# Crossbar transposes for two head pairs of batch 1, and a new order of copies in the prologue, in a fused attention + feed-forward kernel

## The chip, the core and the metric

The kernel runs on one core of one Trainium2 chip. The metric is the device time of one execution in microseconds (us). Every kernel here was executed several times; one execution carries the profile. A profile's *span*, from the first to the last instruction, is about 2 us shorter than the device time of the same execution. A run is called *slow* when it is over 1.5% above the fastest run of the same kernel; slow runs are kept out of the comparisons.

The engines are TensorE (PE in the profile; PEld is its weight load), VectorE (DVE), ScalarE (ACT), GpSimd (POOL) and SyncE (SP; SPq is its queue of DMA issues). Each works through its own list of instructions in a fixed order; the kernel's author chose the orders by hand, so an instruction whose data are late holds up all that stand behind it on that engine.

## The reference

```python
# q, k, v: (4, 8, 768, 64); block = 32, window = 16
k_sum = k.reshape(B, H, nb, block, D).max(axis=3)      # one key per block: the maximum
v_sum = v.reshape(B, H, nb, block, D).mean(axis=3)     # one value per block: the mean
scores_l = scale * q @ k^T          # kept only where |i - j| < 16
scores_s = scale * q @ k_sum^T + log(block)
a = softmax(concat(scores_l masked, scores_s))
x = a @ concat(v, v_sum)            # then (B*S, H*D) = (3072, 512)
h = x @ w_in                        # 512 -> 2048
out = (h * sigmoid(beta * h)) @ w_out   # 2048 -> 512
```

## The kernel before

Heads are worked on in pairs: 4 batches with 4 pairs each. While TensorE does the feed-forward product of batch b (`h_ps`, then `o_ps`), the attention of batch b+1 is slipped in between as "side" work, at positions fixed by numbers. Batch 0's attention is the prologue. For every pair of the next batch the side work is:

1. `copy_v` (a copy of the values on GpSimd) and `prep_v`: the values' block means on TensorE (`vm_ps`), evicted by VectorE (`vm`), and four small copies that SyncE issues as DMAs to put rows and means in place.
2. `transposes`: keys and queries are transposed. Batches 2 and 3 let the DMA crossbar do it (`dma_start_transpose`), issued by SyncE. Batch 1 lets TensorE do it (`pt`), and ScalarE evicts.
3. `rows_a` and `rows_b` on VectorE: the keys' tile `kw` gets extra rows (block maxima `km`, window edges). The crossbar delivers chunks in another order than TensorE's transposes do, so rows after a crossbar transpose take more and smaller copies (the branch `b > 1`).
4. `scores`, `mask`, `av`, `norm` (`x_nat`, VectorE), `x_transpose` (`px`, TensorE in batch 1).

```python
def prep_v(b, g):
    ...                                                    # vm_ps on TensorE
    nc.vector.tensor_copy(out=vm..., in_=...)              # (cut: ScalarE in one case)
    overlaps(b, g, nc.sync)                                # two small DMAs
    eng.dma_start(out=ve[SUM[0]:SUM[0] + nb], in_=vm[:])   # two more; eng is nc.sync
    eng.dma_start(out=vo[SUM[1]:SUM[1] + nb, :, 1:], in_=vm[:])

def transposes(b, g, i):                                   # i = 0 keys, 1 queries
    ...
    if b > 1:
        nc.sync.dma_start_transpose(out=dst, in_=src)
        return
    pt = ps.tile([P, nch, P], bf16, name="pt", tag="t", bufs=2)
    for n in range(nch):
        for h in range(2):
            nc.tensor.transpose(pt[h * D:(h + 1) * D, n], nat[(b, g)][i][:, h * nch + n], identity)
    nc.scalar.copy(out=dst, in_=pt[:])

# the side work of the next batch, for pair g (batch 0 is in its feed-forward part):
t = (16.0, 18.5, 21.5, 24.5)[g]
st, sp, sc_t, av_t = t + 1.3, t - 0.6, (t + 4.6, t + 5.6), t + 9.4
side += [(t - 0.7, copy_v), (t, transposes of keys), (t + 1.2, transposes of queries),
         (st, rows_a and rows_b), (sp, prep_v), (av_t, av), (av_t + 1.2, norm),
         (av_t + 2.3, x_transpose)]                        # (lambdas cut)

# batch 2's loads on GpSimd may not be issued before batch 1's last rows are done:
tc.add_manual_dep(first[(2, 0)].ins, last[(1, npair - 1, "rows")].ins.name, ...)
```

On VectorE, the rows of pair 3 (25.8) stand ahead of the normalisation of pair 0 (26.6). On SyncE, a pair's transposes (t) stand behind its four value copies (t - 0.6). The last line ties batch 2's loads to the rows of pair 3.

The softmax here doesn't subtract the row's maximum and nothing guards it: scores larger than these inputs give would overflow.

## Time and profile before

| | before |
|---|---|
| device time, median of 3 runs | 232.47 us (231.98 to 233.33) |
| span of the profiled run | 230.6 us |
| TensorE busy | 92% of the span |
| first `h_ps` of batch 1 | 87.11 us |
| `px` of pair 0, batch 1 | 72.78 us |
| first load of batch 2 on GpSimd | 71.58 us |

From the page of before: the line of busy time (engine, us, share of the span, instructions), TensorE's busy tenths in 40 slices of the span, and the clock that TensorE was granted in the same slices, in tenths of full speed (9 is 90% or more).

```profile
PE 211.2 (92%) x1969; PEld 118.0 (51%) x1969; DVE 105.6 (46%) x278; ACT 125.4 (54%) x149; POOL 77.1 (33%) x109
PE   0689799997999999999799999999999999999992
PEclk9999999999999999999999999999999999999999
```

TensorE bounds the kernel: after the first slices it is full, so what holds TensorE up costs time, unless a later wait gives some of it back. The waits of TensorE between 45 and 135 us say how little it was held up (instruction, whom it waited for, total us, times, longest):

```profile
PE o_ps L395 <- DVE vm_128 L207: 1.4, 1, 1.4
```

This is the longest. It lies in batch 2 at 114 us. The next longest, 0.9 and 0.8 us, are one for an eviction by ScalarE and one for batch 1's first key load, at 51.5 us.

The timelines have the start, the duration, the engine, the source line, the operation, out<-in, the count, and in brackets the idle time just before with what ended it. SyncE's queue of DMA issues:

```profile
65.46 0.65 SPq L195 DMA_DIRECT2D vo_124<-ve_122  x1
66.19 0.62 SPq L196 DMA_DIRECT2D ve_122<-vo_124  x1
66.90 1.04 SPq L212 DMA_DIRECT2D ve_122<-vm_127  x1
67.99 0.83 SPq L213 DMA_DIRECT2D vo_124<-vm_127  x1
```

These are pair 2's four value copies: each occupies SyncE for 0.6 to 1.0 us just to issue, some 3.5 us for a pair, and SyncE is without a gap from 58.2 us on. VectorE, TensorE and GpSimd at the same time:

```profile
70.82 0.29 DVE L298 COPY kw_120<-km 128x144 bf16<-128x144 bf16 x2
...
71.28 0.96 DVE L350 TENSOR_TENSOR x_nat<-av_ps,r 128x768 bf16<-128x768 f32 x1
```

```profile
71.24 0.35 PE L315 MATMUL s_ps<-q_tr,kw_119 64*128 64x64 bf16 x12
...
72.78 0.51 PE L364 MATMUL px<-identity,x_nat 128*128 128x128 bf16 x6
```

```profile
71.58 1.02 POOL L185 DMA_DIRECT2D ve_121<-in_v_dram  x1 [6.21 <-DVE r L349]
```

Pair 3's rows end at 71.0, the normalisation of pair 0 follows at once, TensorE's `px` follows that without a wait, and GpSimd starts batch 2's loads 0.6 us after pair 3's rows.

### The profile page before, as it was taken

To read this page: it belongs to the slowest core of one execution; us is meant where nothing else is said; L and a number is where in the kernel's file an instruction comes from. 1 tells how busy PE (TensorE), PEld (TensorE's weight loads), DVE (VectorE), ACT (ScalarE), POOL (GpSimd) and SP (SyncE) were. 2 spreads that over 40 slices of the span, in tenths; PEclk is the share of its full clock that TensorE was granted. 3 is DMA by queue.
4 is the path that set the end of the run, shared out by engine and by line. 5 is a ranking of instruction groups with operands and counts; after the bars stand their busy time and mean duration, and the time that the engine had idled before them with its cause. 6 is when DMAs were issued, how large, how long until landed. Compare 5 with 4: busy or idle time off the path is not lost.

```text
span 230.6 us, 4864 instructions
## 1 busy us (share of the span) xinstructions
PE 211.2 (92%) x1969; PEld 118.0 (51%) x1969; DVE 105.6 (46%) x278; ACT 125.4 (54%) x149; POOL 77.1 (33%) x109
## 2 busy tenths in 40 slices
PE   0689799997999999999799999999999999999992
PEld 0456565654545555666344546665445456654441
DVE  4798630545577520598784405766543200002121
ACT  2567886672786537666934237667644177660000
POOL 6999963446415993673560000000000000000000
PEclk9999999999999999999999999999999999999999
DMA  6986599999967999999998339343134410001212
GB/s 177 347 251 145 86 165 205 206 170 156 150 105 104 182 177 210 190 145 141 160 180 158 84 80 173 67 89 62 63 82 110 132 47 0 0 3 45 91 58 80
DMA packets 93254, 29.25 MB, mean 127 GB/s; under 512 B 79792, under 2 KB 89560, under 8 KB 93232
## 3 DMA queue, kind: packets, MB, share of 16 engines
q0 software_dynamic: 61424, 13.76, 69.6%
q1 hardware_dynamic: 28688, 14.02, 27.1%
q10 hardware_dynamic: 3120, 1.18, 1.9%
q8 instruction: 15, 0.25, 0.5%
q14 instruction: 7, 0.06, 0.1%
HBM read 27.27 MB, written 6.29 MB: 146 GB/s over the span
## 4 chain that ended last, share of the span: by engine, by line
PE 64%; DMA 19%; POOL 8%; DVE 3%; SPq 2%; ACT 1%; issue 1%; POOLq 0%; ACTq 0%
PE o_ps L395 34%; PE h_ps L380 23%; DMA k_nat<-in_k_dram 8%; DMA q_tr<-q_nat 4%; DMA w_in_sb<-in_moe_w_in_dram 3%; DMA hold_83<-in_v_dram 3%; PE av_ps L339 3%; PE s_ps L315 2%; POOL ve_121 L175 2%; POOL vo_123 L175 1%; PE pt L251 1%; PE vm_ps L202 1%; POOL hold_83 L81 1%; DVE vm_128 L207 1%; SPq L246 1%
## 5 line engine op out<-in xcount | busy, mean ns | idle before, releaser
L395 PE MATMUL o_ps<-w_out_sb,h_sb 128*128 128x512 bf16 x384 | 88.9, 380 | 1.6 <-DVE vm_128 L207 1.4
L380 PE MATMUL h_ps<-xT,w_in_sb 128*128 128x384 bf16 x512 | 85.5, 326 | 0.1
L384 ACT ACTIVATE h_sb<-h_ps,beta_sb 128x768 bf16<-128x768 f32 x64 | 57.2, 900 | 24.9 <-PE h_ps L380 24.8
L380 PEld LDWEIGHTS <-w_in_sb 128*128 128x128 bf16 x512 | 49.7, 98 | 32.4 <-issue 0.3
L395 PEld LDWEIGHTS <-h_sb 128*128 128x128 bf16 x384 | 35.1, 98 | 40.5 <-issue 1.5
L318 ACT ACTIVATE attn<-s_ps,bias 128x768 bf16<-128x768 f32 x32 | 28.4, 900 | 15.7 <-PE s_ps L315 15.6
L399 DVE COPY o_sb<-o_ps 128x512 f32<-128x512 f32 x6 | 4.2, 692 | 42.1 <-PE o_ps L395 42.1
L399 ACT COPY o_sb<-o_ps 128x512 f32<-128x512 f32 x18 | 10.5, 585 | 23.3 <-PE o_ps L395 21.9
L324 DVE TENSOR_TENSOR attn<-attn,band 128x768 bf16<-128x768 bf16 x24 | 15.2, 638 | 15.3 <-ACT attn L318 15.3
L185 POOL DMA_DIRECT2D k_nat<-in_k_dram x12 | 12.4, 1037 | 11.9 <-DMA kw_120<-k_nat 4.6
L350 DVE TENSOR_TENSOR x_nat<-av_ps,r 128x768 bf16<-128x768 f32 (+1 forms) x17 | 15.4, 910 | 0.6
L185 POOL DMA_DIRECT2D q_nat<-in_q_dram x12 | 12.4, 1032 | 7.5 <-DMA q_tr<-q_nat 3.2
L160 DVE TENSOR_SCALAR w_out_sb<-w_out_sb,inv_beta 128x512 bf16<-128x512 bf16 x16 | 6.1, 436 | 12.9 <-DMA w_out_sb<-in_moe_w_out_dram 12.9
L185 POOL DMA_DIRECT2D ve_122<-in_v_dram x8 | 8.2, 1031 | 4.5 <-DMA w_in_sb<-in_moe_w_in_dram 1.9
L202 PEld LDWEIGHTS <-A_avg 128*128 128x128 bf16 x96 | 7.1, 102 | 5.2 <-issue 3.2
L339 PEld LDWEIGHTS <-attn 128*64 128x64 bf16 x384 | 7.4, 110 | 4.4 <-issue 3.4
L266 DVE COPY kw_117<-kw_117 128x480 bf16<-128x480 bf16 x2 | 0.6, 284 | 19.7 <-DMA kw_117<-k_nat 19.7
L349 DVE RECIPROCAL r<-av_ps 128x12 f32<-128x12 f32 x16 | 3.6, 224 | 11.8 <-PE av_ps L339 11.8
L190 POOL COPY vo_124<-ve_122 128x768 bf16<-128x768 bf16 x8 | 7.2, 894 | 4.9 <-DMA ve_122<-in_v_dram 4.9
L226 PE MATMUL pk<-identity,k_nat 128*128 128x128 bf16 x24 | 3.0, 288 | 6.1 <-POOL k_nat L169 5.9
L365 ACT COPY xT<-px 128x768 bf16<-128x768 bf16 x7 | 5.6, 798 | 3.2 <-PE px L364 3.2
L202 PE MATMUL vm_ps<-ve_121,A_avg 128*128 128x128 bf16 x48 | 4.6, 240 | 2.1 <-POOL ve_121 L175 2.0
(165 smaller groups left out, 201.0 us busy)
## 6 DMA issues: line engine op xcount, KB each, us to landing
out_dram<-o_sb SPq DMA_DIRECT2D x24, 256.0 KB
k_nat<-in_k_dram POOLq DMA_DIRECT2D x12, 192.0 KB, 9.6
q_nat<-in_q_dram POOLq DMA_DIRECT2D x12, 192.0 KB, 10.4
w_out_sb<-in_moe_w_out_dram POOLq DMA_DIRECT2D x4, 512.0 KB, 16.2
w_in_sb<-in_moe_w_in_dram POOLq DMA_DIRECT2D x3, 512.0 KB, 9.9
ve_122<-in_v_dram POOLq DMA_DIRECT2D x8, 192.0 KB, 12.8
hold_81<-in_k_dram POOLq DMA_DIRECT2D x2, 384.0 KB, 5.3
hold_82<-in_q_dram POOLq DMA_DIRECT2D x2, 384.0 KB, 4.8
```

The lines of the kernel that those rows point to most:

```text
L175: copy(out=t[:, :, :, 0:D], in_=f)
L185: ins = nc.gpsimd.dma_start(out=dst, in_=src[b, g])
L190: nc.gpsimd.tensor_copy(out=vo[:, :, 1:, 0:D], in_=ve[:, :, :, 0:D])
L202: nc.tensor.matmul(vm_ps[:], A_avg[:, c, :], ve[:, :, c, 0:D], start=(c == 0), stop=(c == nch - 1))
L318: nc.scalar.activation(out=a.rearrange("p i n q -> p i (n q)"), in_=big[:, :, 0:w], func=ACTF.Exp, bias=bias[:, par:par + 1], scale=scale)
L324: nc.vector.tensor_mul(out=a, in0=a, in1=band[:, par, None, None, :].to_broadcast([P, 2, nch, QT]))
L339: nc.tensor.matmul(o[par * QT:(par + 1) * QT, h, m * HW:(m + 1) * HW], a[:, par, i, n], vt[par][:, h, m], start=True, stop=True)
L350: nc.vector.tensor_mul(out=x_nat[(b, g)][:, lo:hi].rearrange("p m h d -> p h m d"), in0=ov[:, :, lo:hi, 0:D], in1=r_of[(b, g)][:, :, lo:hi ...
L380: nc.tensor.matmul(big[:, kk, 0:MG], w_in_sb[:, ki, ni * P:(ni + 1) * P], xT[b][:, ki, kk * MG:(kk + 1) * MG], start=(ki == 0), stop=(ki = ...
L384: nc.scalar.activation(out=h_bufs[(b, ni // 8)][:, ni % 8, :].rearrange("p (k m) -> p k m", k=2), in_=big[:, :, 0:MG], func=ACTF.Silu, sca ...
L395: nc.tensor.matmul(o_ps[:], h_bufs[(b, ni // 8)][:, ni % 8, ms * P:(ms + 1) * P], w_out_sb[:, ni, :], start=(ni == 0), stop=(ni == k2 - 1))
L399: (nc.scalar.copy if b + 1 < B else nc.vector.tensor_copy)(out=o_sb[:], in_=o_ps[:])
```

## The change

The change has two parts.

*Prologue (batch 0).* The second copy of the keys, which VectorE made with a reduce, is now written by ScalarE straight from PSUM (the memory of the kernel's `ps` tiles, which TensorE's results go to), and pair 0's rows are put ahead of a cast on VectorE. Some later steps of the prologue are reordered.

*Crossbar (batch 1).* Pairs 2 and 3 take the path of batches 2 and 3: SyncE's crossbar transposes instead of 12 TensorE transposes and a ScalarE eviction for each of two tiles of each pair. The intent is to take 48 transposes off the engine that bounds the kernel.

```diff
+        nc.scalar.copy(out=kw_bufs[g][:, 1, :, QT - W:P].rearrange("p m (f e) -> p m f e", e=NE),
+                       in_=pk.rearrange("p e (m f) -> p m f e", f=P // NE)[:, :, (QT - W) // NE:])
 ...
+    def by_parity(b, g):
+
+        return b > 1 or (b == 1 and g >= 2)
 ...                                     # in transposes; the same swap in rows_a, rows_b and av
-        if b > 1:
+        if by_parity(b, g):
             nc.sync.dma_start_transpose(out=dst, in_=src)
 ...
-            if b == 2:
+            if not by_parity(b - 1, g):
                 nc.vector.memset(kv[D:P, 1, :, nj - 1, 0:W], 0.0)
 ...
-            cv(out=kw[:, 1, :, QT - W:P], in_=kw[:, 0, :, QT - W:P])
+            if b:
+                cv(out=kw[:, 1, :, QT - W:P], in_=kw[:, 0, :, QT - W:P])
 ...                                     # the order of the prologue
     pool_0()
-    cast_qk("k", 1, dve)
     prep_k(0)
     prep_q(0)
     rows_a(0, 0)
+    cast_qk("k", 1, dve)
 ...
-    sc(2)
+    scores(0, 2, 0)
+    prep_q(3)
+    scores(0, 2, 1)
+    av(0, 1)
     rows_a(0, 3)
     rows_b(0, 3)
-    prep_q(3)
     sc(3)
-    fin(1)
+    norm(0, 1)
+    av(0, 2)
+    norm(0, 2)
     x_transpose(0, 0)
+    x_transpose(0, 1)
 ...                                     # (two more moved lines cut)
```

More of the change, by code (lines that the diff above doesn't have):

```diff
@@ L262, in rows_a @@
         km = at_pool.tile([P, nb], bf16, name="km", tag="km")
-        if b > 1:
+        if by_parity(b, g):
             kv = kw.rearrange("p r (h j) f -> p r h j f", h=2)
@@ L280, in rows_b @@
         kw, km = kw_bufs[(b * npair + g) % NKW], kms.pop((b, g))
-        if b > 1:
+        if by_parity(b, g):
             kv = kw.rearrange("p r (h j) f -> p r h j f", h=2)
@@ L336, in av @@
             for m in range(nch):
-                i, n = (m % 2, h * nj + m // 2) if b > 1 else (h, m)
+                i, n = (m % 2, h * nj + m // 2) if by_parity(b, g) else (h, m)
                 for par in range(2):
@@ L466 @@
     rows_b(0, 2)
+    prep_k(3)
     fin(0)
-    prep_k(3)
     prep_v(0, 3)
@@ L475 @@
         load_next(1, g)
-    sc(2)
+    scores(0, 2, 0)
+    prep_q(3)
+    scores(0, 2, 1)
+    av(0, 1)
     rows_a(0, 3)
     rows_b(0, 3)
-    prep_q(3)
     sc(3)
-    fin(1)
+    norm(0, 1)
+    av(0, 2)
+    norm(0, 2)
     x_transpose(0, 0)
+    x_transpose(0, 1)
     nc.vector.tensor_copy(out=identity32[:], in_=identity[:])
-    fin(2)
-    x_transpose(0, 1)
     load_beta()
```

## The prediction

> **What bounds the kernel now.** The page's busy table gives TensorE 92% of 230.6 us; by stretches it is full from 70 us to the end but for one 1.4 us wait near 114 us. The chain of waits runs through GpSimd in the head (8 to 26 us), then DMA: a w_in load, and batch 1's first k_nat, which lands at 52.24 us. TensorE's last h_ps matmul of batch 0 ends by 51.0, so the prologue already has slack against that load.
>
> **Prologue part.** Per pair VectorE drops a 128x480 reduce (0.64 us) and ScalarE gains a 480-column copy (estimate 0.56 us, from its 0.59 us for 512). Pair 0's rows no longer stand behind the 1.23 us k cast. I expect h_ps to start 0 to 1 us before 29.35. GpSimd's order does not change, so the loads do not move; k_nat still lands near 52.2 and the gain becomes a longer wait there. Worth: about 0.
>
> **Batch 1 part.** Removed: four groups of 12 TensorE transposes (0.46 us each, 1.85 us), some 0.5 us of waits around them, and four ScalarE copies of 0.80 us. Added: four crossbar transposes on SyncE's queue. In the timeline of before, SyncE issues without a gap from 58.2 to 72.6 us (four value copies per pair, about 3.5 us a pair). The built order puts pair 2's transposes after pair 2's value copies, so they cannot start before about 68.9. In batch 3, with quiet DMA, VectorE could use a transpose 2.8 us after its issue began (147.41 to 150.26), and the rows of this layout take 3.0 us instead of 1.9. In the built order:
> - Pair 2's keys land at 71.7, rows done 74.8. Its first scores (71.24 in before, about 69 without the removed work) wait: a hole of 6 us.
> - VectorE copies pair 3's value means after these rows: 75.7 (68.0 in before).
> - SyncE's copies of those means stand before pair 3's key transpose: issue 77.6, landed 80.4, rows done 83.5.
> - VectorE's normalisation of pair 0 stands behind these rows: x_nat at 84.7. TensorE's px transpose of pair 0 (72.84 in before) waits: a hole of 8 us.
> - From px to batch 1's first h_ps was 14.4 us of full TensorE, so h_ps starts at 99.2 instead of 87.3: +11.9 us.
> - The Trainium skill, "TensorE: Matmul & The Clock Gate", Part 1, says TensorE falls to half rate after an idle window of about 3.4 us and needs as long to recover. In the head of this trace six 128-column transposes take 0.84 us, later 0.49, which agrees. I add 1.5 us, an estimate.
>
> Batch 2's loads wait for pair 3's rows (83.5; loads at 71.6 in before), so they move with h_ps and the rest shifts as a whole.
>
> **Prediction: 245.5 us**, 80% range 239 to 250. Faster by over 2%: 4%; within 2%: 6%; slower: 90%.
>
> **What would show it right.** Waits: s_ps of pair 2 on VectorE's kw rows, px of pair 0 on x_nat, VectorE several us each on the kw_119 and kw_120 transposes. SyncE issues the kw_119 transpose near 69, kw_120 near 77.6. Batch 1's first h_ps near 99 to 101. The k_nat wait at 51 us grows if h_ps starts earlier.
>
> **What would make it wrong.** SyncE reaching pair 2's transposes well before 69; batch 1's loads moving with the prologue; transposes landing much faster or slower than 2.8 us; the clock staying full through the holes (-1.5); slack in batch 2 that takes part of the shift back.

## The result

| | before | after |
|---|---|---|
| device time, median of 4 runs | 232.33 us | 244.64 us |
| lowest and highest | 231.98 to 233.33 | 243.02 to 246.79 (the highest is a slow run) |
| ratio of the means of the fast runs | | 1.0499, 95% interval 1.0434 to 1.0564 |
| span of the profiled run | 230.6 us | 242.8 us |
| mean granted TensorE clock | 0.999 | 0.965 |

A ratio here and below is the mean time of one kernel's fast runs over that of the other's fast runs of the same rounds, so it is not quite the ratio of the medians quoted.

The page of after, the same three lines:

```profile
PE 214.3 (88%) x1921; PEld 119.0 (49%) x1921; DVE 107.2 (44%) x286; ACT 124.3 (51%) x149; POOL 77.0 (32%) x109
PE   0788899997944099999999999999999999999993
PEclk9999999999995569999999999999999999999999
```

48 matmul instructions are gone, yet TensorE's busy time rose by 3 us, and there is a hole in the slices at 67 to 85 us with a low clock in and behind it. The same stretch in the view by windows (window, its length, busy us of PE, PEld, DVE, ACT and POOL with instructions, granted clock, DMA share, GB/s):

```profile
70.00:84.50 14.50, 2.76 (x28) 1.12 (x29) 8.84 (x32) 2.29 (x3) 0.71 (x1) 0.57 0.42 99
```

TensorE worked 2.76 of 14.5 us. Its waits between 45 and 135 us:

```profile
PE px L371 <- DVE x_nat L357: 7.1, 1, 7.1
PE s_ps L322 <- DVE kw L299: 5.0, 1, 5.0
```

The 1.4 us wait of before is not in this list any more. SyncE's queue shows where the holes begin:

```profile
67.81 0.83 SPq L213 DMA_DIRECT2D vo<-vm  x1
68.74 1.32 SPq L252 DMA_TRANSPOSE kw<-k_nat  x1
...
75.60 0.84 SPq L212 DMA_DIRECT2D ve<-vm  x1
76.49 0.82 SPq L213 DMA_DIRECT2D vo<-vm  x1
77.41 1.24 SPq L252 DMA_TRANSPOSE kw<-k_nat  x1
```

and VectorE's timeline how they are passed on:

```profile
71.59 0.28 DVE L272 COPY kw<-kw 128x480 bf16<-128x480 bf16 x1 [6.64 <-DMA kw<-k_nat]
...
74.41 0.30 DVE L299 COPY kw<-kf 128x144 bf16<-128x144 bf16 x2
74.63 0.94 DVE L207 CAST vm<-vm_ps 24x768 bf16<-24x768 f32 x1
...
80.19 0.28 DVE L272 COPY kw<-kw 128x480 bf16<-128x480 bf16 x1 [3.69 <-DMA kw<-k_nat]
...
83.01 0.30 DVE L299 COPY kw<-kf 128x144 bf16<-128x144 bf16 x2
...
83.49 0.96 DVE L357 TENSOR_TENSOR x_nat<-av_ps,r 128x768 bf16<-128x768 f32 x1
```

Read the two together. Pair 2's key transpose is issued at 68.74, behind the value copies; VectorE can use it 2.85 us later, at 71.59, and its rows end at 74.7. Only then comes `vm`, the means of pair 3. Only then (75.60) can SyncE issue the copies of those means, and only behind them (77.41) pair 3's key transpose, which VectorE can use at 80.19. Its rows end at 83.3, and the normalisation of pair 0, whose inputs TensorE had finished by 68.7, comes behind them. So one late transpose makes the next one late, through VectorE's and SyncE's orders in turn. TensorE and GpSimd:

```profile
74.67 0.50 PE L322 MATMUL s_ps<-q_tr,kw 64*128 64x64 bf16 x12 [5.00 <-DVE kw L299]
...
84.50 0.82 PE L371 MATMUL px<-identity,x_nat 128*128 128x128 bf16 x6 [7.08 <-DVE x_nat L357]
...
86.06 3.36 PE L402 MATMUL o_ps<-w_out_sb,h_sb 128*128 128x512 bf16 x8
```

```profile
83.79 1.02 POOL L185 DMA_DIRECT2D ve<-in_v_dram  x1 [19.57 <-DVE r L356]
```

The `px` transposes took 0.82 us where before they took 0.51, and the eight `o_ps` matmuls behind them 3.36 us (1.90 in before): the clock was still low. The view by windows gives it as 0.86 on average from `px` to `h_ps` of batch 1 (1.00 in before):

```profile
84.50:101.00 16.50, 16.50 (x169) 8.65 (x170) 5.48 (x10) 6.06 (x8) 14.42 (x18) 0.86 2.09 146
```

The first `h_ps` of batch 1 starts at 100.92.

The 12.2 us of span are three terms, each a difference of the two timelines:

| stretch | before | after | difference |
|---|---|---|---|
| start to `px` of pair 0 | 72.78 | 84.50 | +11.7 |
| `px` to the first `h_ps` of batch 1 | 14.33 | 16.42 | +2.1 |
| first `h_ps` of batch 1 to the end of the span | 143.5 | 141.9 | -1.6 |

### The profile page after: what moved, and what is told of

Same layout as the page of the kernel before. It is cut to its first block, busy times and chain, and to the rows that moved or that the text cites. A ratio compares the mean times of both kernels' runs of the same rounds, so it can differ in the third digit from the quotient of the medians.

```text
span 242.8 us, 4790 instructions
## 1 busy us (share of the span) xinstructions
PE 214.3 (88%) x1921; PEld 119.0 (49%) x1921; DVE 107.2 (44%) x286; ACT 124.3 (51%) x149; POOL 77.0 (32%) x109
## 4 chain that ended last, share of the span: by engine, by line
PE 48%; DMA 23%; POOL 10%; issue 10%; DVE 6%; SPq 1%; ACT 0%; POOLq 0%
PE o_ps L402 25%; PE h_ps L387 17%; DMA ve<-in_v_dram 8%; DMA w_out_sb<-in_moe_w_out_dram 8%; DMA kw<-k_nat 5%; PE av_ps L346 2%; POOL hold L81 2%; PE s_ps L322 2%; DMA hold<-in_k_dram 2%; POOL q_nat L185 1%; PE vm_ps L202 1%; POOL k_nat L185 1%; POOL w_in_sb L413 1%; DVE km L282 1%; DVE vm L207 1%
## 5 line engine op out<-in xcount | busy, mean ns | idle before, releaser
L402 PE MATMUL o_ps<-w_out_sb,h_sb 128*128 128x512 bf16 x384 | 91.0, 387 | 0.9 <-DVE vm L207 0.6
L402 PEld LDWEIGHTS <-h_sb 128*128 128x128 bf16 x384 | 35.7, 99 | 41.3 <-issue 2.9
L185 POOL DMA_DIRECT2D ve<-in_v_dram x12 | 12.5, 1040 | 24.3 <-DVE r L356 19.6
L272 DVE COPY kw<-kw 128x480 bf16<-128x480 bf16 x10 | 2.8, 278 | 33.6 <-DMA kw<-k_nat 33.6
L207 DVE CAST vm<-vm_ps 24x768 bf16<-24x768 f32 x15 | 14.2, 943 | 7.7 <-PE vm_ps L202 7.7
L322 PEld LDWEIGHTS <-kw 64*128 64x128 bf16 x384 | 8.2, 100 | 17.6 <-issue 5.7
L322 PE MATMUL s_ps<-q_tr,kw 64*128 64x64 bf16 x384 | 12.2, 201 | 5.1 <-DVE kw L299 5.0
L357 DVE TENSOR_TENSOR x_nat<-av_ps,r 128x768 bf16<-128x768 f32 (+1 forms) x17 | 15.4, 910 | 0.6
L282 DVE TENSOR_REDUCE km<-kw 128x24 bf16<-128x768 bf16 x16 | 15.2, 948 | 0.1
L190 POOL COPY vo<-ve 128x768 bf16<-128x768 bf16 x12 | 10.5, 878 | 8.9 <-DMA ve<-in_v_dram 7.0
L202 PE MATMUL vm_ps<-ve,A_avg 128*128 128x128 bf16 x96 | 9.3, 241 | 3.1 <-POOL ve L175 2.1
## 6 DMA issues: line engine op xcount, KB each, us to landing
w_out_sb<-in_moe_w_out_dram POOLq DMA_DIRECT2D x4, 512.0 KB, 15.4
```

What stands on the lines that cost most here:

```text
L185: ins = nc.gpsimd.dma_start(out=dst, in_=src[b, g])
L202: nc.tensor.matmul(vm_ps[:], A_avg[:, c, :], ve[:, :, c, 0:D], start=(c == 0), stop=(c == nch - 1))
L207: (nc.scalar.copy if (b, g) == (0, npair - 1) else nc.vector.tensor_copy)(out=vm[:, :, :, 0:D], in_=mv[:, :, None].to_broadcast([nb, 2, nc ...
L282: nc.vector.tensor_reduce(out=km[:], in_=kw[:, 0].rearrange("p m (n f) -> p (m n) f", f=block), op=ALU.max, axis=mybir.AxisListType.X)
L322: nc.tensor.matmul(big[:, i, n * QT:(n + 1) * QT], kw[i * D:(i + 1) * D, par, n, :], qt[i * D:(i + 1) * D, n, par * QT:(par + 1) * QT], st ...
L357: nc.vector.tensor_mul(out=x_nat[(b, g)][:, lo:hi].rearrange("p m h d -> p h m d"), in0=ov[:, :, lo:hi, 0:D], in1=r_of[(b, g)][:, :, lo:hi ...
```

## The experiments

All gave correct results. Kernels were timed in four sessions, each with its own runs of before, whose medians were 233.3 to 233.6. The texts use letters for theories. Theory Q: the whole loss comes from the crossbar part, because its transposes stand late in SyncE's queue and each makes the next step late. Rival P: the new prologue carries part of it. Rival R: it doesn't matter where the transposes stand, the crossbar path itself costs it. Later two more: theory T says that TensorE's late arrival at batch 1's `h_ps` is what sets the end, theory L that batch 2's loads, released by pair 3's rows and therefore 12.2 us later, set it.

### e1: the prologue part alone

```diff
-        return b > 1 or (b == 1 and g >= 2)      # after
+        return b > 1
```

> The prologue part alone, batch 1 all on TensorE. Theory Q (the time is lost in two holes of batch 1 that come from the order on SyncE's queue and on VectorE): only the prologue's own loss remains, h_ps starts near 30.6 us and of its 1.2 us some 0.8 us gets past the k_nat wait, so 233.0 us (232.3 to 234). Rival P (the reordered prologue delays batch 1 and makes a good part of the loss): 235 us or more.

Measured: ratio 1.0006 (0.9957 to 1.0055), median 233.91. No cost of the prologue is shown; the interval leaves room for about 1 us either way, but not for a good part of 12 us, so P falls. Its profile still shows the first `h_ps` of batch 0 at 30.95 instead of 29.35, as after's had (30.56). The last part of the section on the prediction comes back to that.

### e2: the crossbar part alone

```diff
+    def by_parity(b, g):                          # before, with the four swaps of the change
+        return b > 1 or (b == 1 and g >= 2)
```

> The batch 1 part alone, prologue as before. Theory Q: the chain starts where SyncE has issued pair 2's value copies (near 68.9 us), which the prologue does not move, so both holes stay, px of pair 0 starts near 84.5 and the time is 243.5 to 245 us. Rival P: clearly less, under 241 us.

Measured: ratio 1.0506 (1.0452 to 1.0561), median 245.02; the waits are 5.8 and 7.1 us, `px` is at 83.96. Within that noise the crossbar part is the whole loss.

### e3: after, with the transposes earlier in SyncE's queue

```diff
+                tr = {2: 17.8, 3: 20.8}.get(g, t) if b == 0 else t    # were 21.5 and 24.5
-                (t, lambda g=g: transposes(nxt, g, 0)),
+                (tr, lambda g=g: transposes(nxt, g, 0)),
```

Pair 2's transposes now stand ahead of pair 1's value copies, pair 3's ahead of pair 2's.

> The changed kernel, with pair 2's transposes ahead of pair 1's value copies on SyncE and pair 3's ahead of pair 2's; nothing else is moved. Theory Q: pair 2's keys land near 64.5 and its hole is gone; pair 3's are issued near 68.3 and land near 71.1, x_nat of pair 0 near 75.6 instead of 84.4, so 9 us less: 235.5 us (233 to 237.5). Rival R (the crossbar transposes themselves are slow or crowded by the batch's loads, wherever they stand): they now run beside the loads and land no sooner than before, 241 us or more.

Measured: ratio 1.0172 (1.0113 to 1.0231), median 238.23. The same transposes, moved in the queue, give back two thirds of the loss, so R falls as the whole cause; that the transposes also took longer in their new places is the part of it that stays. The size was missed by 2.7 us. The key transposes took longer than in after: issued at 62.50 and 69.09, used at 66.69 and 73.01, which is 4.2 and 3.9 us instead of 2.85. The first ran beside batch 1's loads (in the view by windows the DMA share, which can go above 1 as it is printed, is 1.94 at 60 to 67 us here, 0.48 at 68 to 75 us in after). The second did not: the share is 0.47 at 67 to 74 us. Its issue alone took 2.38 us, and I don't know why. The hole ahead of pair 2's scores was gone; the one ahead of `px` was still 5.5 us:

```profile
69.09 2.38 SPq L252 DMA_TRANSPOSE kw<-k_nat  x1
```

```profile
77.34 0.82 PE L371 MATMUL px<-identity,x_nat 128*128 128x128 bf16 x6 [5.53 <-DVE x_nat L357]
```

### e4: after, with pair 0's normalisation ahead of pair 3's rows

```diff
-                (av_t + 1.2, lambda g=g: norm(nxt, g)),
+                (av_t + (0.1 if (b, g) == (0, 0) else 1.2), lambda g=g: norm(nxt, g)),
```

> The changed kernel, with VectorE's normalisation of pair 0 ahead of pair 3's rows; SyncE's queue as changed. Theory Q: the first hole stays (scores of pair 2 at 74.7), px of pair 0 starts near 77.5 instead of 84.5, and the next wait is for pair 3's rows at 83.3 by its scores, which started at 89.4: 6 us less, 238.5 us (237 to 240). If the wait of px were due to anything but the order on VectorE, no change (244.6).

Measured: ratio 1.0429 (1.0367 to 1.0492), median 243.99. This missed by 5.5 us, and it taught most. The mechanism worked: `px` was at 76.89, and `h_ps` of batch 1 at 94.65, 6.3 us earlier than in after. But GpSimd started batch 2's loads at 82.97, nearly as late as in after, and TensorE now waited in batch 2, which the list of waits between 66 and 140 us shows:

```profile
PE vm_ps L202 <- DVE vm L207: 2.6, 1, 2.6
PE o_ps L402 <- DVE vm L207: 2.2, 1, 2.2
```

6.3 us won less 4.8 us of new waits would leave 1.5 us. In the profiled runs not even that was left: the spans are 242.9 and 242.8 us, since TensorE was also slow behind the second wait, where eight `o_ps` matmuls took 3.06 us instead of 1.89 and the granted clock was 0.60 (122.2 to 125.3 us):

```profile
122.23 3.06 PE L402 MATMUL o_ps<-w_out_sb,h_sb 128*128 128x512 bf16 x8 [2.23 <-DVE vm L207]
```

The ratios of e4 and after differ by 0.7%, which is 1.6 us, but they come from different sessions and their intervals overlap, so a gain is not shown. So there is a second chain behind the first: pair 3's rows release batch 2's loads, the loads feed batch 2's first transposes and rows, and VectorE evicts the `vm` that TensorE waits for only behind those rows. The next experiments ask which of the two chains binds.

### e15: before, with only batch 2's loads released late

```diff
-            tc.add_manual_dep(first[(2, 0)].ins, last[(1, npair - 1, "rows")].ins.name,
+            tc.add_manual_dep(first[(2, 0)].ins, last[("n", 1, npair - 1)].ins.name,   # last normalisation
```

(Every engine's order is that of before. The position of `load_next` in the text was moved to suit, which changes none.)

> The kernel before, every engine's instructions in the same order; only the wait that releases batch 2's loads is put on the last normalisation of batch 1 (82.9 us) instead of pair 3's rows (71.1). Theory L (what sets the time is when batch 2's loads are released: in the six profiles so far the span is 159.0 to 160.1 us more than the start of the first of them): loads near 83.1, TensorE untouched until batch 2, and still 242.5 us of span, 244 us of time. Theory T (the holes of TensorE in batch 1 set the time): 232 to 234 us, as there are none here.

Measured: ratio 1.0341 (1.0243 to 1.0438), median 241.26. The loads started at 83.61, as in after; `h_ps` of batch 1 at 87.32, as in before. TensorE's timeline in batch 2:

```profile
117.47 0.59 PE L395 MATMUL o_ps<-w_out_sb,h_sb 128*128 128x512 bf16 x1 [7.35 <-DVE vm L207]
```

The result lies between what the two theories expected. Late loads alone, with everything else untouched, cost 3.4%, some 8 us (2.4 to 4.4% by the interval); the waits for `vm` in batch 2 add up to 8.1 us. So the prediction's picture, in which the loads only move along, is incomplete: it suggests that with TensorE's holes filled and the loads still late, much of the loss would stay.

### e11: after, with the loads released by pair 2's rows

```diff
-            tc.add_manual_dep(first[(2, 0)].ins, last[(1, npair - 1, "rows")].ins.name,
+            tc.add_manual_dep(first[(2, 0)].ins, last[(1, npair - 2, "rows")].ins.name,
```

> The changed kernel with batch 2's loads released by pair 2's rows (74.6 us) instead of pair 3's (83.3). Theory L alone: the first load starts near 75 and the time falls by 8 us to 236. Both chains (the holes of TensorE alone are long enough too): h_ps of batch 1 still starts at 101 us or later, so 242 to 246 us, the upper end if the earlier loads crowd pair 3's transpose.

Measured: ratio 1.0699 (1.0616 to 1.0781), median 250.37, the worst of all. The loads started at 75.69, 8 us earlier than in after, and that did not help at all. They met pair 3's transpose, as SyncE's and VectorE's timelines show:

```profile
77.90 1.26 SPq L252 DMA_TRANSPOSE kw<-k_nat  x1
```

```profile
84.89 0.29 DVE L272 COPY kw<-kw 128x480 bf16<-128x480 bf16 x1 [7.89 <-DMA kw<-k_nat]
```

The transpose that took 2.8 us in after took 7.0 us here, beside the loads (the DMA share is 1.63 at 76 to 86 us, against 0.48 at 68 to 75 us in after), and `px` came at 89.62. L alone falls, and the manual dependency is shown to earn its place in the changed kernel. In before it is not: there e14, below, finds no cost of releasing the loads earlier.

### e6: after, with TensorE kept busy in the second hole

```diff
+        if (b, g) == (1, 0):
+            dm = ps.tile([P, d_model], f32, name="dm", tag="t", bufs=2)
+            for _ in range(16):                    # results are not used
+                nc.tensor.matmul(dm[:], identity, w_out_sb[:, 0, :], start=True, stop=True)
         px = ps.tile([P, S], bf16, name="px", tag="t", bufs=2)
```

> The changed kernel with 16 matmuls of 512 columns, their result unused, ahead of px of pair 0, inside the second hole. If the slow TensorE after the hole is due to its idling, px to h_ps takes 14.4 us instead of 16.4 and h_ps starts near 98.9. Theory L: the loads of batch 2 do not move, the 2 us come back as a wait in batch 2, and the time falls by 0.5 us or less (244.1). Theory T: it falls by 2 us (242.6).

Measured: ratio 1.041 (1.0334 to 1.0486), median 243.63. TensorE's timeline:

```profile
77.34 4.76 PE L372 MATMUL dm<-w_out_sb,identity 128*128 128x512 bf16 x16
84.48 0.51 PE L375 MATMUL px<-identity,x_nat 128*128 128x128 bf16 x6 [2.38 <-DVE x_nat L357]
```

`px` started at the same time as in after, and took 0.51 us again. From `px` to `h_ps` it was 14.34 us, where before takes 14.33. So the 2.1 us that after takes longer were the clock. The view by windows has the granted clock, just ahead of its last two figures:

```profile
77.00:82.20 5.20, 5.11 (x28) 2.00 (x28) 1.94 (x7) 1.39 (x2) 0.00 (x0) 0.74 0.59 141
...
84.50:99.00 14.50, 14.24 (x167) 7.83 (x171) 5.45 (x10) 6.05 (x8) 14.32 (x18) 1.00 2.08 148
```

The first hole, 5.8 us here, had already lowered it. The useless matmuls began at the low clock (0.56 at 77.3 to 80 us) and brought it back (1.00 from 80 us on). This is what the Trainium skill, "TensorE: Matmul & The Clock Gate", Part 1, says of an idle window of about 3.4 us, after which TensorE runs at half rate until it has been busy for as long: the two waits of after, 5.0 and 7.1 us, are longer than that, the granted clock in the window was 0.57, and the 2.38 us of idle time that were left behind the 16 useless matmuls did not lower it again. (Shorter waits are not always harmless: in e4 two of 2.6 and 2.2 us within 7 us were followed by a clock of 0.60, and in e16, below, one of 3.75 us by 0.70.) Against after's ratio of 1.0499, from another session, it fell by 0.9%, which is 2 us; the two intervals overlap, so the profiles carry the reading: with the loads where they were (83.77), the span fell from 242.8 to 241.0 us. So in after TensorE's chain is the one that binds, and the loads' chain is close behind: the wait in batch 2 is back with 0.2 us, so that an estimate for its distance is 2.1 - 0.2 = 1.9 us.

### e13: both pairs early, normalisation first, loads released early

The old prologue, both pairs' transposes at 17.8, ahead of pair 1's value copies (in e3 only pair 2's stood there), the normalisation of e4 and the dependency of e11 together.

```diff
+                tr = {2: 17.8, 3: 17.85}.get(g, t) if b == 0 else t            # in e3: 17.8, 20.8
+                (av_t + (0.1 if (b, g) == (0, 0) else 1.2), lambda g=g: norm(nxt, g)),   # as e4
+            ... last[(1, npair - 2, "rows")].ins.name,                          # as e11
```

> A repaired version: the prologue of before, the crossbar for pairs 2 and 3 of batch 1, both pairs' transposes ahead of pair 1's value copies on SyncE, pair 0's normalisation ahead of pair 3's rows, batch 2's loads released by pair 2's rows. Both chains are served: loads near 70 us (71.6 in before), h_ps of batch 1 near 87, no wait of TensorE in batch 2: 231 us (229.5 to 233), ratio 0.993. If the crossbar is crowded by the loads of batch 1 and 2: 234 or more.

Measured: ratio 1.015 (1.0063 to 1.0237), median 237.52. Missed by 6.5 us. The transposes were early enough, but GpSimd issued batch 2's loads from 69.95 on, while VectorE did pair 3's rows. VectorE's timeline:

```profile
72.32 0.78 DVE L270 COPY kw<-kw 128x480 bf16<-128x480 bf16 x1
...
73.31 0.70 DVE L272 COPY kw<-kw 64x64 bf16<-64x64 bf16 x1
...
74.03 0.95 DVE L279 TENSOR_REDUCE km<-kw 128x24 bf16<-128x768 bf16 x1
...
76.03 2.00 DVE L294 COPY kf<-km 64x24 bf16<-64x24 bf16 x4
```

The same copies and reduce in after took 0.28, 0.18, 0.95 and 0.71 us (in the order shown). Rows that take 3.0 us took 6.0, TensorE waited 3.0 us for them, and the clock fell again. Four groups of copies slow down, those of L288 from 0.18 to 0.81 us among them; others and the reduce do not. The Trainium skill, "SBUF — State Buffer", section "Who interferes with whom", states something that fits: a VectorE copy that uses both ports shares them with GpSimd, and whoever comes first blocks the other; a `tensor_reduce` never contends. No trace shows the ports themselves. That the traffic of the loads slows the copies, and not GpSimd, can be excluded from the traces. In the fourteen of them, 1206 copies of rows ran while GpSimd was idle, 330 of these at a DMA share of 1.5 or more, and none took over 1.1 times the median of its shape; of the 420 that ran beside an instruction of GpSimd, 118 took over 1.5 times that. The reduces took 0.93 to 0.96 us in all 224 cases.

### e8: e13 with the loads released by pair 3's rows again

```diff
-            ... last[(1, npair - 2, "rows")].ins.name,     # e13
+            ... last[(1, npair - 1, "rows")].ins.name,
```

> The repaired version of the run before, but with batch 2's loads released by pair 3's rows again, as in both kernels. If what spoilt that version is that VectorE's rows and normalisations ran beside GpSimd's issue of the loads: pair 3's rows now take 3.0 us and end near 75.6, its scores start near 75.7 instead of 78.3, h_ps of batch 1 near 86, the loads near 76.4, and the late loads cost what is left: span 233 us, ratio 1.008 (0.998 to 1.018). If the crossbar itself was the cause: 1.015 or more and rows of pair 3 as late as before.

Measured: ratio 1.0143 (1.0058 to 1.0229), median 237.54, one of four runs slow. The number is within what was expected, and too near to 1.015 to decide; the rows decide. Pair 3's rows took 3.0 us again (72.98 to 76.0), which agrees with the reading of e13, as the only edit is when GpSimd issues the loads:

```profile
73.46 0.18 DVE L272 COPY kw<-kw 64x64 bf16<-64x64 bf16 x1
...
75.05 0.71 DVE L294 COPY kf<-km 64x24 bf16<-64x24 bf16 x4
```

`h_ps` of batch 1, expected near 86, was at 89.39, 2.3 us later than in before; the loads at 76.58, 5 us later, and TensorE waited 1.05 and 2.08 us for `vm` in batch 2. So even with the best order that I found for both pairs, pair 3's rows come 5 us later than before, and the loads' chain collects it.

### e5: after, with pair 3's value means ahead of pair 2's rows on VectorE

```diff
-                    st, sp, sc_t, av_t = t + 1.3, t - 0.6, ...
+                    st, sp, sc_t, av_t = t + 1.3, t - (1.8 if g == 3 else 0.6), ...   # and copy_v likewise
```

> The changed kernel, with pair 3's value means copied by VectorE ahead of pair 2's rows. If SyncE's copy of these means holds back pair 3's key transpose behind it: that copy starts near 73.5 instead of 75.6, the transpose near 75.3 instead of 77.4, pair 3's rows end near 81.2, and loads and px are 2.1 us earlier, as both chains start there: ratio 1.041. If not: 1.050.

Measured: ratio 1.0399 (1.0298 to 1.0501) from the three fast runs of six; the profiled run was slow, so only its order of events is used. SyncE issued the two key transposes at 69.94 and 76.52, which is 6.6 us apart instead of 8.7 in after: the 2.1 us that were expected of taking `vm` out of the chain. This agrees with the reading of the queue. The starting points were missed, though: pair 2's transpose itself was issued 1.2 us later than in after, so pair 3's came 0.9 us earlier and not 2.1, and `px` at 83.65 instead of 84.50. So that the ratio is the expected one (1.041) is in part luck, and with three slow runs the time alone would not carry the reading.

### e14: before, with the loads released by pair 2's rows

```diff
-            tc.add_manual_dep(first[(2, 0)].ins, last[(1, npair - 1, "rows")].ins.name,
+            tc.add_manual_dep(first[(2, 0)].ins, last[(1, npair - 2, "rows")].ins.name,
```

> The kernel before with batch 2's loads released by pair 2's rows (67.1 us) instead of pair 3's (71.1). The only wait of TensorE in batch 2 (1.4 us) should shrink, worth 1 us at most; against it, VectorE's rows and normalisations of pair 3 run beside GpSimd's issue of the loads. Ratio 0.995 to 1.005; above 1.005 if that crowding costs more than the wait.

Measured: ratio 0.9971 (0.9901 to 1.0042), median 232.76. The loads started at 67.47, 4.1 us earlier, and the wait in batch 2 shrank only from 1.4 to 1.0 us. No gain is shown. It is a second look at VectorE beside GpSimd's issues: the same copies of pair 3's rows took 0.80 and 0.77 us here (0.18 and 0.29 in before).

### e16: the crossbar for pair 2 alone, early

```diff
-        return b > 1 or (b == 1 and g >= 2)                                     # e2
+        return b > 1 or (b == 1 and g == 2)
+                tr = {2: 17.8, 3: 24.5}.get(g, t) if b == 0 else t
```

> The prologue of before; the crossbar for pair 2 of batch 1 alone, its transposes ahead of pair 1's value copies on SyncE; pair 3 on TensorE as before. TensorE loses 1.1 us of work and waits, VectorE gains 1.1 us of rows ahead of pair 3's rows, so batch 2's loads are released some 2 us later than in before (near 74 instead of 71.6). If the release of the loads sets the time, the saving is given back: ratio 1.003 (0.997 to 1.010). If TensorE's work in batch 1 does: 0.995.

Measured with five rounds: ratio 1.0097 (1.0045 to 1.0149), median 235.71. The time is at the edge of what was expected, but not for a reason that I had named. One pair's transposes less, and TensorE still lost; VectorE's and TensorE's timelines:

```profile
70.00 0.94 DVE L207 CAST vm<-vm_ps 24x768 bf16<-24x768 f32 x1
```

```profile
71.00 0.53 PE L255 MATMUL pt<-identity,k_nat 128*64 128x128 bf16 x12 [3.75 <-DVE vm L207]
```

The transposes of pair 3, on TensorE in this kernel, need a PSUM buffer that `vm_ps` holds, and VectorE evicts that only at 70.00, behind pair 2's rows, which wait for the crossbar until 66.96, 4.4 us after the issue. The wait of 3.75 us is the same fault in a new place, and the clock fell behind it (0.70 granted at 71 to 74 us, 0.80 at 74 to 78). No version was faster than the kernel before, clear of noise.

### How far ahead of TensorE the loads start

The profiles of these runs can be laid side by side (e5's is slow and left out). The lead is the time from the first load of batch 2 to the first `h_ps` of batch 1; the wait is what TensorE then waited for `vm` in batch 2.

| kernel | first load | first `h_ps` | lead | waits in batch 2 |
|---|---|---|---|---|
| e15 | 83.61 | 87.32 | 3.7 | 8.1 |
| e4 | 82.97 | 94.65 | 11.7 | 4.8 |
| e8 | 76.58 | 89.39 | 12.8 | 3.1 |
| e6 | 83.77 | 98.82 | 15.1 | 0.2 |
| e1 | 72.67 | 88.10 | 15.4 | 2.1 |
| before | 71.58 | 87.11 | 15.5 | 1.4 |
| e3 | 76.62 | 93.30 | 16.7 | 1.2 |
| e16 | 74.58 | 91.64 | 17.1 | 0 |
| after | 83.79 | 100.92 | 17.1 | 0 |
| e2 | 83.24 | 101.06 | 17.8 | 0 |
| e14 | 67.47 | 87.12 | 19.7 | 1.0 |
| e13 | 69.95 | 93.33 | 23.4 | 1.5 |
| e11 | 75.69 | 105.71 | 30.0 | 0 |

With a lead under 15 us the wait grows steeply. Over that it is 0 to 2.1 us, and the lead alone does not say which: e14 and e13, with more lead than after, still wait. So it is shown that after lost the wait of 1.4 us which before has, and with it nearly all of the 1.6 us of the third term; that its longer lead is the cause fits most rows and is not proved. (The 0.6 us that after has for `o_ps` on `vm` lies at 53 us, in batch 1, and is not counted.)

## Why the prediction was right, and where it was not

The time was right, 245.5 against 244.64, and so was the account of the holes, which are the bulk of it. Two smaller terms were wrong in opposite directions (the clock, +0.6 us, and the rest of the kernel, -1.6 us), so part of the closeness is luck. Step by step:

| step as predicted | predicted | measured |
|---|---|---|
| SyncE reaches pair 2's key transpose | 68.9 | 68.74 |
| VectorE can use it after | 2.8 us | 2.85 us |
| rows of pair 2 done | 74.8 | 74.7 |
| hole ahead of pair 2's scores | 6 us | 5.0 us |
| pair 3's key transpose issued | 77.6 | 77.41 |
| rows of pair 3 done | 83.5 | 83.3 |
| hole ahead of `px` of pair 0 | 8 us | 7.1 us |
| `px` of pair 0 | 84.7 | 84.50 |
| clock after the holes | +1.5 us | +2.1 us (e6) |
| first `h_ps` of batch 1 | 99.2, and the clock's 1.5 | 100.92 |
| prologue, first `h_ps` of batch 0 | 0 to 1 us earlier | 1.2 us later in this profile |
| the rest "shifts as a whole" | 0 | -1.6 us |

*The holes.* Everything between 68 and 85 us came as predicted, because each duration was taken from the same trace: a transpose's 2.8 us and the rows' 3.0 us from batch 3, SyncE's issue times from batch 1, and the orders from the built program. The holes were each 1 us shorter than predicted, but ended when predicted; in e2, with the old prologue, the first was 5.8 us, since TensorE came to it earlier. e2 shows that this part is all of the loss within the noise, e3 that the place in the queue and not the crossbar is the cause of most of it.

*The clock term* was mis-sized: 2.1 us instead of 1.5, as e6 shows.

*"The rest shifts as a whole"* failed. The shift was given back by 1.6 us, since the wait of 1.4 us that before had in batch 2 was not there any more. The prediction named such slack among the things that would make it wrong.

*The loads "move with h_ps"* was true of the times, but it hid a second chain. e15 shows that the loads' delay alone costs some 8 us, and e4 that of the 6.3 us that a remedy for TensorE's hole alone won at `h_ps` nothing was left in the profiled run (1.6 us by the ratios, not clear of noise). My expectation of e4, 5.5 us too low, made the same error, and had to be wrong before I saw it. In after TensorE's chain binds and the loads' chain lies some 1.9 us behind (e6).

*The prologue* was right in worth (about 0; e1 gives 1.0006) and wrong in sign in the profile of after. Seven profiled kernels have the new prologue, the same program up to that point: their first `h_ps` of batch 0 starts at 29.15 (e11), 29.70 (e6), 29.71 (e4), and at 30.56 (after), 30.86 (e5), 30.95 (e1) and 31.17 (e3). In the late ones groups of TensorE instructions that take 0.49 to 0.51 us at full speed still took over 0.8 us at 22 to 23 us; in e11 they were at full speed from 18.5 us on. Of the seven with the old prologue all start between 29.02 and 29.93. So the best case of the new prologue (29.15) is no earlier than the best of the old (29.02): no gain of the reordering is shown. The late starts go with when TensorE's clock is let up. The Trainium skill, "TensorE: Matmul & The Clock Gate", Part 1, says that the window runs free and that the warm-up varies from run to run, with which these seven agree. Why the new prologue is late in four of seven and the old in none is not settled. It cost nothing that the ratios can show (e1): in before TensorE waits 0.8 us for batch 1's first key load at 51.5 us, and in e1 and after that wait is gone. In e1's profile 1.0 of the 1.6 us was still there at `h_ps` of batch 1 (88.10 against 87.11), too little for its interval; in after the hole ahead of pair 2's scores takes up whatever is left.

## What to carry to other kernels

Taking work off the busiest engine was worth nothing here, because the replacement stood in an in-order queue behind other things: find the place in the built order, and follow each engine's order from there, since finished work (here a normalisation) can be caught behind late work (here rows). Before a time is put on a delay, look for everything that the delayed instruction releases, loads above all; delay that alone in the old kernel, as e15 does, and see what it costs. And an idle stretch of some microseconds on TensorE has a second price, the low clock behind it, which a few idle matmuls can measure.

## What the Trainium skill lacked or had wrong

- "DMA: Bandwidth & Descriptors", section "Anatomy of one DMA", gives a fixed cost of about 2.0 us for a DMA on GpSimd's path, and "VectorE: DVE Perf Modes", section "The three transpose paths", 1309 ns for one 128x128 transpose on the crossbar. Neither page says how long after its issue a larger transpose can be used: here one of 128x768 from SBUF to SBUF could be used 2.8 us after its issue began with quiet DMA (after), 3.9 to 4.7 us where it was issued at 62 to 69 us (e3, e8, e13, e16), and 7.0 us beside loads (e11).
- The same page, "DMA: Bandwidth & Descriptors", gives what an issue costs SyncE only in cycles, in a comparison with another chip (512 for a copy in "previous generations"), not in time. Here SyncE was occupied for 0.6 to 1.0 us by most small copies (one took 1.65 us, in after) and for 1.2 to 1.3 us by most 128x768 crossbar transposes (before and after), with one of 2.38 us (e3). In an in-order queue these add up.
- "SBUF — State Buffer", section "Who interferes with whom", says that VectorE copies and GpSimd can exclude each other and that a reduce takes no part, which these runs fit. Its practical advice is about loads starved by VectorE; for the converse it has one factor ("DVE 6.8× slower") without the case. These runs give one: copies of 0.18 us took 0.70 to 0.81 us, and rows of 3.0 us took 6.0 us, while GpSimd issued loads (e13 against e8). VectorE's copies on a critical chain should be kept apart from GpSimd's issues.
- "TensorE: Matmul & The Clock Gate", Part 1, agrees with these runs on long holes: 5.0 and 7.1 us, then 2.1 us lost, and nothing lost where 2.4 us of idle time were left (e6). But two waits of 2.6 and 2.2 us close together were followed by a clock of 0.60 (e4), so here a wait under 3.4 us was not safe by itself. The page warns that the clock's events in a trace can be unreliable; a case of it is that the granted clock is full before 18 us in before, where groups of six 128-column transposes took 0.82 to 0.84 us that later take 0.49 to 0.51 us.
